# A decode step of attention beside a gated MLP, with gradients: the MLP's w2 in 18 blocks of 96 rows, and the first head's loads and products ahead of the MLP

## The chip, the cores and the metric

The kernel runs on one core of a Trainium2 chip, in one launch. The metric is the time of one execution on the device in microseconds (us). Three runs of the kernel before took 762.09, 760.68 and 760.85 us; the median is 760.85 us.

## The reference, cut to what matters

One token (`Sq = 1`, width `D = 640`) passes a layer norm without gain. Two branches read the result and are added to the input: attention over a cache of 8192 keys and values for each of 32 heads of width 128, and a gated MLP of inner width `F = 1728`. The kernel returns the output and the gradients with respect to the input, both caches and all five weights. All arrays are bfloat16.

```python
def _fwd_reference(A_x, A_k_cache, A_v_cache, A_wq, A_wo, B_x, B_w1, B_w3, B_w2):
    xn = _layernorm(A_x)
    q = (xn @ wq)                                  # 32 heads of 128
    p = softmax(q . k_cache * 128 ** -0.5)         # 8192 keys a head
    attention = (p . v_cache) @ wo
    h = silu(xn @ w1) * (xn @ w3)                  # 1728 wide
    return A_x + attention + h @ w2
# reference(): out, and the vjp of it with grad_out for
#   A_x, A_k_cache, A_v_cache, A_wq, A_wo, B_w1, B_w3, B_w2
```

With one token every weight gradient is an outer product of two vectors, and so is the gradient of each head's K and V. The kernel therefore reads every large array once and writes an array of the same size for each: 151.34 MB in and 151.34 MB out by the profile.

## The kernel before

Every large tile in SBUF has 128 partitions; a head's K or V is one tile of 2 MB (128 partitions of 64 rows of 128 values). The work is in three stretches.

Setup. `x_row` and `g_row` are loaded, constants are made, and the layer norm is done. `nc.sync` (the SP queue) issues all loads in the order of the program: w1 (L142), w3 (L144), w2 in three parts (L149), then `load_wq(0)` (L130), `load_wo(0)` (L137), `load_k(0)` (L108), `load_v(0)` and `load_v(1)` (L114).

The gated MLP, `mlp_steps()`, a generator that stops once at its `yield`. In the first part TensorE forms gate and up as 16 + 16 columns of `gu_ps` (L448: for each of w1 and w3, 16 blocks of 108 columns by 5 chunks of 128 rows, each block being the stationary operand). VectorE multiplies each part of w2 with the gradient (`T2`, L459), TensorE adds it up over pieces of 64 columns with an identity (`dh_ps`, L462), and VectorE ends the sum (L455). A chain of small operations on `sm_f` gives the gradients of gate and up; `diag` (L486) spreads them over a diagonal. Between the two parts the kernel runs `prep_steps(0)`, which makes q and the gradient of the attention output for the first four heads (`qs_g`, `do_g`). In the second part a product with ones turns `diag` into rows that all partitions hold (`bc_sb`, L496 to L502). Then four things follow: the MLP output (L509), the gradient of w2, written over `w2c` by ScalarE (L511) and stored by `nc.gpsimd` (the POOL queue, L512); the products of w1 and w3 with `bc_sb` for the gradient of x (`T`, L518, summed by L521); and the gradients of w1 and w3, which VectorE writes over the weights themselves (L524) before POOL stores them (L528).

The heads. The loop runs from -1 to 31. In iteration h the next head n = h + 1 gets its scores and its products with V: `product(n, "S", 0/1)` and `product(n, "DP", 0/1)`, each half a VectorE product (L333) and eight matmuls with the identity that add it up (L335); `row_max` and `exps` between them. The current head c = h gets its probabilities (`probs`), its outer products (`outer`, L342 on VectorE and L346 on ScalarE, each stored by POOL, L348), `attend`, `dscores` and its share of the weight gradients. For iteration -1 only the part for head 0 runs. `load_v(h + 2)` and `load_k(h + 3)` stand inside the loop.

The order on VectorE, ScalarE, SP and POOL is the order of the program (`manual_schedule`); TensorE's instructions are placed by the scheduler and then run in that order. What the loads must wait for is set by the pools:

- `kpool` has three buffers. They hold w1, w3 and K of head 0 first. `load_k(1)` takes the buffer of w1, and so it waits until the gradient of w1, which stands in that buffer, has been stored. `load_k(2)` waits in the same way for the store of the gradient of w3.
- `vpool` has two buffers, for V of heads 0 and 1. `load_v(2)` waits until head 0 is done with V.
- `opool` has seven buffers: the three parts of w2, `diag`, `bc_sb`, and later the outer products `ot`.
- `tpool` has two buffers, for all products that TensorE sums up (`T2`, `T13` and `T`).

The order at the start of the loop before the change is:

```python
        mlp = mlp_steps()
        next(mlp)
        for _ in prep_steps(0):
            pass
        for _ in mlp:
            pass
        load_k(1)
        load_k(2)
        prev = None
        for h in range(-1, H):
```

Of the kernel before, what the change touches and what calls it, by code (L numbers as in the profile page):

```python
# [9 lines left out]
BF16 = mybir.dt.bfloat16  # L10
F32 = mybir.dt.float32
# [5 lines left out]
P = 128  # L17
# [4 lines left out]
def kernel(  # L22
# [22 lines left out]
    nc = tc.nc  # L45
# [3 lines left out]
    D = A_x.shape[2]  # L49
# [8 lines left out]
    ORDERED = {mybir.EngineType.DVE, mybir.EngineType.SP, mybir.EngineType.Pool, mybir.EngineType.Activation}  # L58
    GW = 8
    HB = GW // GH  # L60
    R2 = 16
    FR = F // R2
    ACT_J = 8
    assert H % GW == 0 and GW % GH == 0 and F % R2 == 0 and FR <= P and P % GH == 0
# [8 lines left out]
    opool = ctx.enter_context(tc.tile_pool(name="op", bufs=7))  # L73
# [16 lines left out]
    w1_v = B_w1.rearrange("(p ci) f -> p ci f", ci=NC)  # L90
# [6 lines left out]
    with tc.manual_schedule(engines=ORDERED):  # L97
# [8 lines left out]
        def load_k(h):  # L106
            Kt = kpool.tile([P, J, DH], BF16, name="Kt", tag="K")
            nc.sync.dma_start(Kt[:], kc[h])  # L108
            kv_tiles[h] = kv_tiles.get(h, [None, None])
            kv_tiles[h][0] = Kt  # L110

        def load_v(h):
            Vt = vpool.tile([P, J, DH], BF16, name="Vt", tag="V")
            nc.sync.dma_start(Vt[:], vc[h])  # L114
            kv_tiles[h] = kv_tiles.get(h, [None, None])
            kv_tiles[h][1] = Vt
# [22 lines left out]


        w1t = kpool.tile([P, NC, F], BF16, name="w1t", tag="K")
        nc.sync.dma_start(w1t[:], w1_v)  # L142
        w3t = kpool.tile([P, NC, F], BF16, name="w3t", tag="K")
        nc.sync.dma_start(w3t[:], w3_v)  # L144
        w2_parts = []
        r0 = 0
        for rows in (6, 5, 5):
            w2c = opool.tile([P, rows, D], BF16, name="w2c", tag="o")
            nc.sync.dma_start(w2c[0:FR], w2_v[:, r0:r0 + rows, :])  # L149
            w2_parts.append((r0, rows, w2c))  # L150
            r0 += rows
        assert r0 == R2
        load_wq(0)
        load_wo(0)
        load_k(0)
        load_v(0)
        load_v(1)


# [277 lines left out]
                steps.append(finish_steps(st.g))  # L437


        def mlp_steps():  # L440
            DRUN = 64
            DR1 = 96
            assert F % DR1 == 0 and D % DRUN == 0
# [44 lines left out]
                                    .to_broadcast([FR, 2, R2, FR // 2, 2]),  # L488
                                    dgu2[0:FR].unsqueeze(3).to_broadcast([FR, 2, R2, FR // 2, 2]), ALU.mult)
            bc_sb = opool.tile([P, 2, F], BF16, name="bc_sb", tag="o")  # L490
            yield
            RC = 4
            for wi in range(2):
                for r0 in range(0, R2, RC):
                    bc_ps = ps_w.tile([P, RC, FR], F32, name="bc_ps", tag="w")
                    nc.tensor.matmul(bc_ps[:], lhsT=ones_bf[0:FR, :],  # L496
                                     rhs=diag[0:FR, wi, r0:r0 + RC].rearrange("p r a b -> p r (a b)"), start=True, stop=True)
                    part = bc_sb[:, wi, r0 * FR:(r0 + RC) * FR].rearrange("p (r q) -> p r q", r=RC)
                    if wi == 0 and r0 % (2 * RC) == 0:
                        nc.vector.tensor_copy(part, bc_ps[:])  # L500
                    else:
                        nc.scalar.copy(part, bc_ps[:])  # L502
# [32 lines left out]
            if steps and next(steps[0], "end") == "end":  # L535
                steps.pop(0)

        mlp = mlp_steps()
        next(mlp)
        for _ in prep_steps(0):  # L540
            pass
        for _ in mlp:
            pass
        load_k(1)
        load_k(2)
        prev = None
        for h in range(-1, H):
            n = new_head(h + 1) if h + 1 < H else None
            c = hs.pop(h) if h >= 0 else None
            if h >= 0:  # L550
                g, hh = divmod(h, GH)
            if h == H - 2:
                for dst, src in late:
                    store(dst, src)
            if n:
                product(n, "S", 0)
            if c:
                probs(c)
                outer(c, c.do, c.P2, c.Pf, dvc, h, 0)
                if prev:  # L560
                    keep_dq(prev)
                gap()
                row_dots(c)
                attend(c)
                turn_wq(c)
            if n:
                product(n, "S", 1)
            if c:
                outer(c, c.do, c.P2, c.Pf, dvc, h, 1)
                if h + 2 < H:  # L570
                    load_v(h + 2)
                gap()
                dscores(c)
                outer(c, c.q, c.U2, c.Uf, dkc, h, 0)
                keep_wq(c)
            if n:
                row_max(n)
                product(n, "DP", 0)
            if c:
                outer(c, c.q, c.U2, c.Uf, dkc, h, 1)  # L580
                if h + 3 < H:
                    load_k(h + 3)
                gap()
            if n:
                exps(n)
                product(n, "DP", 1)
            if c:
                weights(c)
                gap()
                if hh == 0 and g + 1 < NG:  # L590
                    if (g + 1) % HB == 0:
                        load_wq((g + 1) // HB)
                    load_wo(g + 1)
                if hh == 1 and g + 1 < NG:
                    steps.append(prep_steps(g + 1))
                    gap()
                if hh == 2:
                    gap()
            prev = c
        keep_dq(prev)  # L600
        while steps:
            gap()
# [58 lines left out]
```

## Time and profile before

| What | Value |
|---|---|
| Median of three runs | 760.85 us |
| The profiled execution's own time | 761.41 us |
| Its span, first to last instruction | 759.4 us |
| PE (matmuls) busy | 557.3 us, 73% of the span |
| DVE (VectorE) busy | 632.5 us, 83% |
| ACT (ScalarE) busy | 474.4 us, 62% |
| POOL (GpSimd) busy | 87.5 us, 12% |
| Moved by DMA | 303.72 MB, mean 400 GB/s |
| Mean granted TensorE clock | 0.79 of full speed |
| Loads of w1 and w3 | 2160 KB each |
| Loads of w2 | 810 + 675 + 675 KB |
| Loads of wq (eight heads) and wo (four heads) | 1280 KB and 640 KB |
| Load of one head's K or V | 2048 KB |

The span lies 2.0 us under the execution's own time. A busy share is a mean over the three stretches, which have different limits; the stretches are seen in the page's row of 40 slices, of about 19 us each. A timeline gives for each group of instructions its start, the time to the end of the group, the engine ("SPq" and "POOLq" are queues that issue transfers, "PEld" is TensorE's loading of a stationary operand), the line, and what it reads and writes.

### The profile page before, as it was taken

Reading aid. Unit: us, or ns where it says so; the run is one execution under the profiler, and the core shown is the slowest. Engines: PE = TensorE matmul, PEld = TensorE weight load, DVE = VectorE, ACT = ScalarE, POOL = GpSimd, SP = SyncE. Lnnn points to the kernel's source line nnn. Section 1 sums busy time; section 2 is a strip of 40 time slices with the busy share of each in tenths; the row PEclk is TensorE's granted clock in tenths of the full one; section 3 lists DMA queues with packets and bytes.
Section 4 is the critical chain, followed back from the end, with each engine's and each line's share of the span. In section 5 each row is a group of like instructions: output and inputs, shape, how many; then the busy total and the mean of one; then the engine's idle time right before and its main releaser. Section 6 shows DMA issues by size and latency. Waiting matters only on the chain.

```text
span 759.4 us, 15976 instructions
## 1 busy us (share of the span) xinstructions
PE 557.3 (73%) x6528; PEld 337.3 (44%) x6543; DVE 632.5 (83%) x706; ACT 474.4 (62%) x1421; POOL 87.5 (12%) x166
## 2 busy tenths in 40 slices
PE   6865888878688773877777765788786778777860
PEld 5652445544454442544443433444353445444440
DVE  2577999999799894998788994999887998899970
ACT  2180567777666763787655963778564957677672
POOL 0010011111001120110100120111000111011120
PEclk9987778787886687787896987777795888877665
DMA  8969799999999999999999999999999999999795
GB/s 298 335 258 366 301 428 425 423 422 418 430 427 428 423 416 426 426 423 417 429 428 426 426 377 430 424 427 419 430 425 427 428 418 427 428 427 424 325 363 201
DMA packets 37355, 303.72 MB, mean 400 GB/s; under 512 B 4120, under 2 KB 5874, under 8 KB 12194
## 3 DMA queue, kind: packets, MB, share of 16 engines
q1 hardware_dynamic: 15190, 151.35, 48.5%
q0 software_dynamic: 22080, 151.35, 48.4%
q8 instruction: 51, 0.84, 0.4%
q14 instruction: 22, 0.18, 0.1%
q10 hardware_dynamic: 12, 0.00, 0.0%
HBM read 151.34 MB, written 151.34 MB: 399 GB/s over the span
## 4 chain that ended last, share of the span: by engine, by line
DMA 55%; DVE 31%; PE 6%; issue 4%; ACT 2%; SPq 1%; POOL 0%; POOLq 0%; DVEq 0%; ACTq 0%
DMA out_dram<-ot 39%; DVE T L333 14%; DVE ot L342 11%; DMA out_dram<-wo_g 9%; DMA wo_g<-in_A_wo_dram 4%; DMA w2c<-in_B_w_dram 3%; PE psS L335 2%; ACT ot L346 1%; DVE S_sb L352 1%; DVE DP_sb L386 1%; PE psDP L335 1%; PE dx_ps L521 1%; DVE w3t L524 1%; DVE T L518 1%; SPq L149 0%
## 5 line engine op out<-in xcount | busy, mean ns | idle before, releaser
L335 PE MATMUL psDP<-T,ident_bf 128*128 128x512 bf16 x512 | 187.2, 529 | 65.3 <-DVE T L333 65.3
L335 PEld LDWEIGHTS <-ident_bf 128*128 128x128 bf16 x1024 | 120.2, 120 | 221.8 <-issue 167.0
L346 ACT ACTIVATE ot<-qs_g,Uf 128x128 bf16<-128x128 bf16 x512 | 156.4, 389 | 68.6 <-DMA out_dram<-ot 55.9
L346 ACT ACTIVATE ot<-do_g,Pf 128x128 bf16<-128x128 bf16 x512 | 156.3, 389 | 13.4 <-DMA out_dram<-ot 12.5
L333 DVE TENSOR_TENSOR T<-Kt,qs_g 128x4096 bf16<-128x4096 bf16 x64 | 146.4, 2289 | 2.4 <-PE psDP L335 1.3
L335 PE MATMUL psS<-T,ident_bf 128*128 128x512 bf16 x512 | 141.2, 426 | 9.4 <-DVE T L333 9.4
L333 DVE TENSOR_TENSOR T<-Vt,do_g 128x4096 bf16<-128x4096 bf16 x64 | 146.0, 2281 | 1.4 <-DMA Vt<-in_A_v_cache_dram 1.4
L342 DVE TENSOR_TENSOR ot<-qs_g,U 128x3072 bf16<-128x3072 bf16 x64 | 112.2, 1753 | 40.5 <-DMA out_dram<-ot 40.5
L348 POOL DMA_DIRECT2D out_dram<-ot x128 | 68.2, 533 | 546.3 <-ACT ot L346 192.8
L342 DVE TENSOR_TENSOR ot<-do_g,P 128x3072 bf16<-128x3072 bf16 x64 | 112.3, 1755 | 4.5 <-DMA out_dram<-ot 3.4
L399 PEld LDWEIGHTS <-Kt 128*128 128x128 bf16 x2048 | 57.2, 97 | 12.0 <-issue 9.3
L399 PE MATMUL ob<-U,Kt 128*128 128x1 bf16 x2048 | 57.2, 164 | 2.5 <-issue 1.2
L379 PEld LDWEIGHTS <-Vt 128*128 128x128 bf16 x2048 | 57.1, 97 | 0.0
L379 PE MATMUL ob<-P,Vt 128*128 128x1 bf16 x2048 | 56.9, 163 | 0.0
L365 PEld LDWEIGHTS sm<-rsum,ones_f 128*128 128x128 f32 x64 | 16.4, 282 | 52.7 <-ACT E L364 47.2
L364 ACT ACTIVATE E<-S_sb,negM 128x64 f32<-128x64 f32 x32 | 11.0, 343 | 44.8 <-DVE negM L361 44.7
L245 ACT COPY woT<-ps_t 128x512 bf16<-128x512 bf16 x40 | 22.8, 576 | 25.9 <-PE ps_t L240 25.9
L418 ACT ACTIVATE dq_diag<-ident_bf,odq 128x128 bf16<-128x128 bf16 x32 | 12.8, 399 | 41.2 <-DVE odq L414 41.2
L356 PE MATMUL sm<-ident_f,mrow 128*128 128x128 f32 x64 | 17.6, 361 | 23.8 <-DVE mrow L354 23.0
L373 ACT ACTIVATE Pf<-E,rZ 128x16 f32<-128x16 f32 x32 | 9.8, 307 | 39.2 <-DVE rZ L369 39.2
L352 DVE TENSOR_REDUCE S_sb<-psS 128x64 f32<-128x512 f32 x32 | 21.9, 685 | 11.2 <-PE psS L335 11.2
L262 PE MATMUL ps_d<-woT,G_rep 128*128 128x512 bf16 x33 | 13.4, 405 | 22.6 <-ACT woT L245 22.6
(145 smaller groups left out, 542.4 us busy)
## 6 DMA issues: line engine op xcount, KB each, us to landing
out_dram<-ot POOLq DMA_DIRECT2D x128, 1024.0 KB, 28.4
Kt<-in_A_k_cache_dram SPq DMA_DIRECT2D x32, 2048.0 KB, 17.6
Vt<-in_A_v_cache_dram SPq DMA_DIRECT2D x32, 2048.0 KB, 14.0
wq_g<-in_A_wq_dram SPq DMA_DIRECT2D x4, 1280.0 KB, 24.2
wo_g<-in_A_wo_dram SPq DMA_DIRECT2D x8, 640.0 KB, 9.9
out_dram<-wo_g POOLq DMA_DIRECT2D x8, 640.0 KB, 23.9
out_dram<-wq_g POOLq DMA_DIRECT2D x15, 256.0 KB, 20.4
w1t<-in_B_w_dram SPq DMA_DIRECT2D x1, 2160.0 KB, 8.3
```

The lines of the kernel that those rows point to most:

```text
L245: nc.scalar.copy(woT[:], ps_t[:])
L262: nc.tensor.matmul(ps_d[:], lhsT=G_rep[:, ci, :], rhs=woT[:], start=(ci == 0), stop=(ci == NC - 1))
L333: nc.vector.tensor_tensor(T[:], src[:, :, ds_], vec[:, ds_].unsqueeze(1).to_broadcast([P, J, DHH]), ALU.mult)
L335: nc.tensor.matmul(ps[:], lhsT=ident_bf[:], rhs=T[:, :, RUN * i:RUN * (i + 1)], start=(half == 0 and i == 0), stop=(half == 1 and i == DHH ...
L342: nc.vector.tensor_tensor(ot[:, 0:JD], vec.rearrange("p (a b) -> p a b", b=2).unsqueeze(1).to_broadcast([P, JD, DH // 2, 2]), w2[:, j0:j0 ...
L346: nc.scalar.activation(ot[:, j].rearrange("p a b -> p (a b)"), vec, ACTF.Copy, scale=wf[:, half, j - JD:j - JD + 1])
L348: nc.gpsimd.dma_start(dst[h][:, j0:j0 + JH, :], ot[:].rearrange("p j a b -> p j (a b)"))
L352: nc.vector.tensor_reduce(st.S[:], st.ps["S"][:], AX.X, ALU.add)
L356: nc.tensor.matmul(st.sm[:, 8:8 + P], lhsT=mrow[:].to_broadcast([P, P]), rhs=ident_f[:], start=True, stop=True, skip_group_check=True)
L365: nc.tensor.matmul(st.sm[:, 3:4], lhsT=ones_f[:], rhs=rsum[:], start=True, stop=True, skip_group_check=True)
L379: mm = nc.tensor.matmul(st.ob[:, 0:1], lhsT=st.V[:, j, :], rhs=st.P2[:, j, 0:1], start=(j == 0), stop=(j == J - 1), skip_group_check=True)
L399: nc.tensor.matmul(st.ob[:, 1:2], lhsT=st.K[:, j, :], rhs=st.U2[:, j, 0:1], start=(j == 0), stop=(j == J - 1), skip_group_check=True)
```

## The change

w2 is cut into 18 blocks of 96 rows in place of 16 blocks of 108, so its tiles have 96 partitions; its three parts hold 6 blocks each. The blocks of w1 and w3 in L448 become 96 columns wide. The order of the first loads on the SP queue becomes wq, wo, K of head 0, V of head 0, w2, w1, w3, V of head 1. `prep_steps(0)` and iteration -1 of the head loop (the products and exponents of head 0) come ahead of the MLP, which is one plain function now; the loads of K for heads 1 and 2 follow it as before.

```diff
-    R2 = 16
+    R2 = 18
     FR = F // R2
...
         w1t = kpool.tile([P, NC, F], BF16, name="w1t", tag="K")
-        nc.sync.dma_start(w1t[:], w1_v)
         w3t = kpool.tile([P, NC, F], BF16, name="w3t", tag="K")
-        nc.sync.dma_start(w3t[:], w3_v)
-        w2_parts = []
-        r0 = 0
-        for rows in (6, 5, 5):
-            w2c = opool.tile([P, rows, D], BF16, name="w2c", tag="o")
-            nc.sync.dma_start(w2c[0:FR], w2_v[:, r0:r0 + rows, :])
-            w2_parts.append((r0, rows, w2c))
-            r0 += rows
-        assert r0 == R2
         load_wq(0)
         load_wo(0)
         load_k(0)
         load_v(0)
+        w2_parts = []
+        RP = 6
+        assert R2 % RP == 0
+        for r0 in range(0, R2, RP):
+            w2c = opool.tile([P, RP, D], BF16, name="w2c", tag="o")
+            nc.sync.dma_start(w2c[0:FR], w2_v[:, r0:r0 + RP, :])
+            w2_parts.append((r0, RP, w2c))
+        nc.sync.dma_start(w1t[:], w1_v)
+        nc.sync.dma_start(w3t[:], w3_v)
         load_v(1)
...
-        def mlp_steps():
+        def mlp():
...
             bc_sb = opool.tile([P, 2, F], BF16, name="bc_sb", tag="o")
-            yield
-            RC = 4
             for wi in range(2):
-                for r0 in range(0, R2, RC):
-                    bc_ps = ps_w.tile([P, RC, FR], F32, name="bc_ps", tag="w")
+                for k, (r0, n) in enumerate(((0, 5), (5, 5), (10, 4), (14, 4))):
+                    bc_ps = ps_w.tile([P, n, FR], F32, name="bc_ps", tag="w")
...
-        mlp = mlp_steps()
-        next(mlp)
         for _ in prep_steps(0):
             pass
-        for _ in mlp:
-            pass
-        load_k(1)
-        load_k(2)
         prev = None
         for h in range(-1, H):
...
             prev = c
+            if h < 0:
+                mlp()
+                load_k(1)
+                load_k(2)
```

## The prediction

> **What bounds the kernel now.** I read the page's row of 40 slices first.
>
> ```profile
> DMA  8969799999999999999999999999999999999795
> GB/s 298 335 258 366 301 428 425 423 422 418 430 427 428 423 416 426 426 423 417 429 428 426 426 377 430 424 427 419 430 425 427 428 418 427 428 427 424 325 363 201
> ```
>
> From the sixth slice (95 us) to the 37th the transfers run at about 425 GB/s with a busy share of 9 tenths or more: there the kernel is bound by moving bytes. Only the first five slices and the last three fall short. The first five carry 298 + 335 + 258 + 366 + 301 = 1558 where 5 x 425 = 2125 would fit; the missing 567 x 19 us / 425 are some 25 us. The change touches only this stretch, so I read next the table of windows there (busy time of PE, PEld, DVE, ACT, POOL; granted clock; DMA share; GB/s).
>
> ```profile
> 2.00:12.00 10.00, 5.08 (x53) 4.33 (x54) 4.07 (x17) 4.15 (x6) 0.00 (x0) 1.00 0.99 389
> 14.00:28.00 14.00, 14.00 (x126) 12.91 (x126) 4.09 (x3) 0.00 (x0) 0.00 (x0) 1.00 1.02 233
> 28.00:40.00 12.00, 8.54 (x54) 5.41 (x54) 7.80 (x18) 5.37 (x10) 0.00 (x0) 1.00 1.03 424
> 46.00:58.00 12.00, 7.13 (x78) 6.75 (x76) 10.67 (x6) 7.51 (x11) 3.52 (x4) 0.84 0.62 193
> 58.00:80.00 22.00, 12.93 (x53) 5.41 (x51) 16.72 (x10) 0.44 (x2) 0.57 (x1) 0.70 0.99 385
> ```
>
> The last row is left for what follows. From 14 to 28 us, when w2 lands, the DMA is busy but moves only 233 GB/s; from 46 to 58 us it has too little to do; from 58 to 80 us it is full. Then the SP queue's own waits up to 200 us, and the timeline of the first 85 us:
>
> ```profile
> SPq L108 <- DMA out_dram<-w1t: 42.4, 1, 42.4
> SPq L108 <- DMA out_dram<-w3t: 7.2, 1, 7.2
> ```
>
> ```profile
> 16.89 7.59 PEld L448 LDWEIGHTS <-w3t 128*108 128x108 bf16 x80
> 30.98 1.52 PE L462 MATMUL dh_ps<-T,ident_bf 108*108 108x320 bf16 x10 [1.01 <-DVE T L459]
> 40.42 3.82 DVE L518 TENSOR_TENSOR T<-w1t,bc_sb 128x3456 bf16<-128x3456 bf16 x2
> 41.02 1.85 PEld L509 LDWEIGHTS <-w2c 108*128 108x128 bf16 x65
> 54.74 0.57 POOL L528 DMA_DIRECT2D out_dram<-w1t  x1
> 62.84 4.48 DVE L333 TENSOR_TENSOR T<-Kt,qs_g 128x4096 bf16<-128x4096 bf16 x2
> 66.06 7.99 SPq L108 DMA_DIRECT2D Kt<-in_A_k_cache_dram  x2
> 78.11 2.29 DVE L333 TENSOR_TENSOR T<-Kt,qs_g 128x4096 bf16<-128x4096 bf16 x1 [1.26 <-PE psDP L335]
> ```
>
> The load of K of head 1 waits 42.4 us for the store of the gradient of w1, whose buffer it takes. That store is issued at 54.74 us, the load at 66.06 us. Meanwhile (62.84 to 78.11 us) VectorE does head 0's products. At 78.11 us head 1's first product starts, without a wait for its K. So those 15.3 us of products lie beside the stores of both gradients and the loads of K, while the DMA is full: they cost little.
>
> **My measure.** From head 1's first product on, both programs do the same with the same buffers, and V of head 1 and both gradients of w1 and w3 are out of the way or in flight. The change in time is the shift of this instant, S1 (78.11 us before). DMA-bound or not, what follows moves with it.
>
> **The change part by part.**
>
> *Loads.* In MB the new order is wq 1.31, wo 0.66, K 2.10, V 2.10, w2 2.21, w1 2.21, w3 2.21, V 2.10. The first 10 us at 389 GB/s move 3.89 MB, to 12.0 us; K of head 0 needs 4.07 MB, so 12.4 us. V (6.17 MB) at 424 GB/s ends at 17.4 us. For w2 in 96 partitions no row exists. Its 2.21 MB take 5.2 us at 424 GB/s and 9.5 us at the 233 GB/s of its own stretch; pieces of 1280 bytes stay, so I take 8 us, nearer the slow end: 25.4 us. w1 and w3 add 5.2 us each: 30.6 and 35.8 us. A landing is counted by its last piece; w3 lands in the trace at 1.55 + 14.0 = 15.6 us, where the bytes alone give 13.4, so the lag is 0 to 2.2 us; I take 1. K 13.4, w1 31.6, w3 36.8 us.
>
> The Trainium skill ("DMA: Bandwidth & Descriptors", section "Why a DMA increments its semaphore by 16 and not by 1") says that a transfer is spread over the largest number up to 16 of engines that divides the outer dimension: 12 for 108 partitions, 16 for 96. By it w2 would take 9.5 x 12/16 = 7.1 us and the sum would be 0.9 us lower; it speaks for this part of the change.
>
> *Head 0 first.* `prep_steps(0)` (5.4 us of ACT, before at 33 to 39 us) now lies under the load of K; without that cover it would be 5 us more. The products took from 62.84 us to the end of the last psDP matmul at 81.2 us, 18.3 us; from 13.4 us that gives 31.7 us, when w1 lands. The Exp table (1.28 us) is hidden behind VectorE's products.
>
> *MLP front, TensorE.* In the order of the changed program TensorE has, after head 0: 90 matmuls of w1, 21 of dh, 90 of w3, 9 of dh. Before, the 160 gate and up matmuls lay under the slow load of w2; now w1 and w3 land last and nothing is left to cover them. Their pitch is 7.59 us / 80 = 95 ns with 108 columns; L509 with 128 columns goes at 1.85/65 = 28 ns. 96 columns has no row: 28 and 95 ns bound it; being a width other than 128, I take 95 x 96/108 = 85 ns. 90 are 7.65 us. One dh matmul of 384 is 1.52/10 x 384/320 = 0.18 us. Step by step: w1 to 39.4; 20 dh to 43.0; meanwhile the third w2 product needs the first dh group's buffer (41.2), the reduction (0.56) and itself (2.16, as the first had): 43.9, its first dh matmul 44.1; w3 to 51.8; 9 dh 53.4; reduction 54.0. From the copy of gate and up to the first `T` of L518 were 32.94 to 40.42, 7.5 us, with a ScalarE copy (`do_g`, 1.3 us) in the way that is now gone: 7.0. The new blocks of `bc_ps` (5, 5, 4, 4) change copies by under 0.1 us. L518 starts at 61.0 us, 20.6 later than 40.42.
>
> The skill's page "TensorE: Matmul & The Clock Gate" (section "Weight-path perf modes — Fast Weight Load (FWL) and DoubleRow") gives the fast weight load to 128 columns alone, which speaks against a gain at 96; its formula of columns / 1.2 GHz would make 80 ns, and the sum 0.9 us lower.
>
> *MLP tail.* VectorE's 22.4 us (40.42 to 62.84) stay. POOL stores w1's gradient behind the three of w2, which wait for ScalarE: 18 scalings in place of 16, 2 x 0.73 us more. So 54.74 - 40.42 + 1.5 = 15.8 us after L518: 76.8 us. The 10 more L509 matmuls (0.3 us) lie under VectorE.
>
> *The wait that now shows.* K of head 1 needs the stores of both gradients ahead of it on the engines: 2.21 + 2.21 + 2.10 MB at 385 GB/s are 16.9 us, some 2 more until the first piece: 19 us after the issue. From above, K was there by 78.11, 23.4 us after. I take 21: S1 = 97.8 us. VectorE is done with the MLP at 61.0 + 22.4 = 83.4 and idles 14 us, queued behind this product: `probs`, `outer` and with them all stores of head 0, V of head 2 on SP. The DMA has nothing from 41 us (V of head 1 landed) to the first w2 store at some 67 us.
>
> **Sum.** S1 moves by 97.8 - 78.1 = 19.7, say 20 us. Span 759.4 + 20 = 779.4; own time 761.41 + 20 = 781.4; that execution lies 0.6 us above the median 760.85, so 781 us. With the ends (w2 -2.8 / +1.5, matmul pitch 80 to 95 ns -0.9 / +1.8, lag 1, K -2 / +2.4) the case reaches from 774 to 787.
>
> **Rivals.**
> (a) *Weights of 96 columns load fast.* For: 28 ns at L509. Against: 95 ns at L448 and width alone differs. 90 matmuls take 2.5 us; 5.15 x 2 = 10.3 less: S1 moves 9.5 us, 770.
> (b) *w2 stays slow, or TensorE is throttled when the MLP starts.* For: the granted clock was 0.70 from 58 to 80 us, 1.00 in the 108-column matmuls. w2 as slow as its whole 14 us is 6 more: 787; a clock of one half for both sets of 90 would add up to 15.
> (c) *Faster: bytes alone decide.* The 14 us at 233 GB/s moved 3.26 MB, which need 7.7 us at 424: 6.3 less, 754.5. It holds if computing never starves the DMA, so S1 by 71.8 and L518 by 35.0 us, before w3 has landed (36.8). Merely to break even L518 must start by 41.3. For it speaks that 15.3 us of products leave the stretch after the MLP; against it that they were covered there.
>
> **How the numbers follow.** Main case 0.73, (a) 0.10, (b) 0.12, (c) 0.04, something that ends level 0.01. Under 0.2% (1.5 us) a measurement of this kernel cannot tell from no change. Slower 0.95, same 0.01, faster 0.04. The time is the main case's 781; the range of 769 to 788 takes in (a) and the near end of (b).
>
> **What would show it.** In the new profile: w2 at over 233 GB/s; L447 (gate and up) at 80 to 95 ns; L515's first `T` near 61 us; POOL's store of w1's gradient near 77; VectorE idle some 14 us until K lands; head 1's first product near 98; a hole in the DMA from about 42 to 66 us. It is wrong if that product starts before 80 us, or if the later stretch does not move with it.

## The result, and the profile after

The changed kernel takes 786.38 us (784.18 to 787.23, 4 runs), the kernel before 761.32 us beside it; the ratio is 1.0324, with a 95% interval of 1.0299 to 1.035. The profiled execution took 787.23 us, its span is 785.1 us, 25.7 us longer than before. The page's row of 40 slices (19.6 us each) of the changed kernel:

```profile
DMA  8921889999999999999999999999999999999896
GB/s 322 318 120 39 319 332 419 424 425 423 420 429 427 429 421 420 427 427 422 418 428 429 423 415 394 428 429 425 417 433 427 426 422 415 427 427 414 342 366 201
```

Only the first six slices differ much; the third and fourth (39 to 78 us) are nearly empty; I call that stretch the hole. The timeline of the changed kernel (start, time to the end of the group, engine, line, operation):

```profile
16.26 4.49 DVE L332 TENSOR_TENSOR T<-Kt,qs_g 128x4096 bf16<-128x4096 bf16 x2 [8.68 <-DMA Kt<-in_A_k_cache_dram]
...
38.30 7.36 PE L447 MATMUL gu_ps<-xn_col_bf,w1t 128*96 128x1 bf16 x90 [8.09 <-DMA w1t<-in_B_w_dram]
...
45.52 6.45 PE L461 MATMUL dh_ps<-T,ident_bf 96*96 96x384 bf16 x21
...
51.81 5.29 PE L447 MATMUL gu_ps<-xn_col_bf,w3t 128*96 128x1 bf16 x90
...
56.96 3.09 PE L461 MATMUL dh_ps<-T,ident_bf 96*96 96x384 bf16 x9
...
67.23 3.83 DVE L515 TENSOR_TENSOR T<-w1t,bc_sb 128x3456 bf16<-128x3456 bf16 x2 [0.17 <-ACT bc_sb L499]
...
82.85 0.58 POOL L525 DMA_DIRECT2D out_dram<-w1t  x1
...
92.63 7.03 SPq L108 DMA_DIRECT2D Kt<-in_A_k_cache_dram  x2
...
103.84 2.29 DVE L332 TENSOR_TENSOR T<-Kt,qs_g 128x4096 bf16<-128x4096 bf16 x1 [13.71 <-DMA Kt<-in_A_k_cache_dram]
```

The first `T` of w1 stands at 67.23 us (40.42 before). VectorE idles 13.71 us for K of head 1, and head 1's first product, S1, starts at 103.84, 25.73 us later than before. The SP queue's waits up to 200 us of the changed kernel (total, times, longest, us) show the load of K of head 1 waiting 69.8 us for the store of w1's gradient, in place of 42.4:

```profile
SPq L108 <- DMA out_dram<-w1t: 69.8, 1, 69.8
SPq L108 <- DMA out_dram<-w3t: 6.3, 1, 6.3
```

The same six stretches of both traces follow (busy time of PE, PEld, DVE, ACT, POOL; granted clock; DMA share; GB/s). Before:

```profile
0.00:20.00 20.00, 13.08 (x139) 12.33 (x140) 5.31 (x25) 4.86 (x6) 1.14 (x8) 1.00 0.85 295
20.00:41.00 21.00, 17.26 (x130) 12.87 (x131) 12.56 (x23) 6.37 (x12) 0.00 (x0) 1.00 1.05 354
41.00:60.00 19.00, 13.00 (x186) 12.28 (x183) 16.07 (x8) 12.51 (x19) 3.52 (x4) 0.82 0.69 237
60.00:80.00 20.00, 12.05 (x33) 4.64 (x33) 14.72 (x10) 0.44 (x2) 0.57 (x1) 0.67 0.99 388
80.00:100.00 20.00, 16.17 (x187) 9.20 (x185) 19.58 (x24) 12.15 (x41) 2.13 (x4) 0.82 0.81 310
100.00:120.00 20.00, 16.79 (x187) 9.30 (x187) 19.72 (x21) 12.92 (x45) 2.13 (x4) 0.83 1.00 424
```

After:

```profile
0.00:20.00 20.00, 9.53 (x63) 5.33 (x64) 8.77 (x26) 9.38 (x13) 1.14 (x8) 1.00 0.87 320
20.00:41.00 21.00, 9.43 (x65) 5.55 (x63) 10.39 (x8) 0.44 (x2) 0.00 (x0) 0.83 1.05 328
41.00:60.00 19.00, 19.00 (x179) 15.43 (x179) 3.17 (x3) 0.00 (x0) 0.00 (x0) 0.59 0.20 86
60.00:80.00 20.00, 11.89 (x158) 9.45 (x157) 15.93 (x22) 14.05 (x23) 1.63 (x2) 0.63 0.18 51
80.00:100.00 20.00, 5.55 (x54) 5.25 (x54) 9.30 (x5) 1.83 (x3) 1.85 (x3) 0.71 0.92 342
100.00:120.00 20.00, 11.17 (x153) 6.45 (x153) 15.98 (x17) 10.46 (x34) 1.60 (x3) 0.67 0.83 324
```

I call the *lost DMA time* of a stretch its length times (1 - rate/425), 425 GB/s being the rate of the full stretch. Before it is 6.1 + 3.5 + 8.4 + 1.7 + 5.4 + 0.0 = 25.2 us; after, 4.9 + 4.8 + 15.2 + 17.6 + 3.9 + 4.8 = 51.2. The difference is 25.9 us, and the span grew by 25.7. Of these 25.9 us, 22.6 lie between 41 and 80 us, where the changed kernel has soon loaded all that it may load and has for long nothing to store (the windows of 5 us from 50 to 75 us show 0 to 5 GB/s); 4.7 lie behind 100 us; between 80 and 100 us, where VectorE idles for K, the DMA is at 0.92 and loses less than before.

So two measures fit: the shift of S1, which the prediction used, and the lost DMA time. That the second one fits is in part bookkeeping: every kernel here but e9 moves the same bytes, so its span is these bytes at 425 GB/s plus all its lost DMA time, and the table only adds that what is lost later hardly differs. Which of the two prices a wait rightly is told by the experiments that move S1 and the lost DMA time by different amounts (e6, e10, e12). This table has all twelve experiments, below the change; shifts of the profiled span, of lost DMA time up to 120 us (160 us for the contiguous w2) and of S1 are against the kernel before, in us.

| Kernel | Time, ratio [interval] | Span | Lost DMA time | S1 |
|---|---|---|---|---|
| the change | 786.38, 1.0324 [1.0299, 1.035] | +25.7 | +25.9 | +25.7 |
| e1 blocks only | 760.30, 0.9996 [0.9985, 1.0007] | -0.1 | -0.6 | -0.5 |
| e2 order only | 786.39, 1.0328 [1.0305, 1.0352] | +25.7 | +26.3 | +26.1 |
| e3 loads first only | 788.89, 1.0367 [1.0348, 1.0385] | +27.9 | +27.7 | +27.9 |
| e4 products first only | 794.93, 1.0444 [1.0417, 1.0472] | +35.3 | +34.1 | +35.4 |
| e5 w2 contiguous | 813.34, 1.0695 [1.0674, 1.0717] | +50.9 | +52.2 | +51.9 |
| e6 K's own buffer | 782.90, 1.0301 [1.0269, 1.0333] | +20.4 | +17.4 | +12.6 |
| e7 w2's store later | 787.27, 1.0347 [1.032, 1.0375] | +23.4 | +23.8 | +21.1 |
| e8 half the products | 760.32, 0.9997 [0.9987, 1.0006] | -1.0 | -1.2 | -1.2 |
| e9 w2 in 128 partitions | 782.99, 1.0287 [1.0269, 1.0305] | +22.4 | +20.9 | +22.6 |
| e10 K in place of V | 783.28, 1.0298 [1.0281, 1.0314] | +22.1 | +23.0 | +13.4 |
| e11 added matmuls | 765.89, 1.0067 [1.0055, 1.008] | +4.7 | +4.9 | +4.7 |
| e12 hole filled | 757.05, 0.9938 [0.9924, 0.9952] | -2.7 | -3.5 | +0.8 |

(e9 moves 0.74 MB more, 1.7 us at 425 GB/s; with them its 20.9 are 22.6.)

### The profile page after: what moved, and what is told of

Read it like the earlier page. It is cut to its first block, busy times and chain, and to the rows that moved or that the text cites. A ratio compares the mean times of both kernels' runs of the same rounds, so it can differ in the third digit from the quotient of the medians.

```text
span 785.1 us, 16039 instructions
## 1 busy us (share of the span) xinstructions
PE 556.6 (71%) x6559; PEld 335.7 (43%) x6573; DVE 633.2 (81%) x706; ACT 476.3 (61%) x1423; POOL 86.9 (11%) x166
## 4 chain that ended last, share of the span: by engine, by line
DMA 51%; DVE 33%; issue 9%; PE 3%; ACT 1%; POOL 0%; SPq 0%; POOLq 0%; DVEq 0%; ACTq 0%
DMA out_dram<-ot 29%; DVE T L332 15%; DVE ot L341 13%; DMA out_dram<-wo_g 10%; DMA Kt<-in_A_k_cache_dram 4%; DMA wo_g<-in_A_wo_dram 4%; DMA w2c<-in_B_w_dram 3%; PE psS L334 2%; DVE S_sb L351 1%; DMA out_dram<-w1t 1%; DVE DP_sb L385 1%; ACT ot L345 1%; DVE U L393 1%; DVE P L370 0%; PE psDP L334 0%
## 5 line engine op out<-in xcount | busy, mean ns | idle before, releaser
L334 PE MATMUL psDP<-T,ident_bf 128*128 128x512 bf16 x512 | 175.2, 501 | 68.1 <-DVE T L332 68.1
L334 PE MATMUL psS<-T,ident_bf 128*128 128x512 bf16 x512 | 147.1, 439 | 25.4 <-DVE T L332 25.3
L345 ACT ACTIVATE ot<-do_g,Pf 128x128 bf16<-128x128 bf16 x512 | 156.4, 389 | 13.6 <-DMA out_dram<-ot 12.7
L398 PEld LDWEIGHTS <-Kt 128*128 128x128 bf16 x2048 | 57.3, 98 | 12.6 <-issue 10.0
L364 PEld LDWEIGHTS sm<-rsum,ones_f 128*128 128x128 f32 x64 | 14.2, 242 | 49.6 <-ACT E L363 44.7
L351 DVE TENSOR_REDUCE S_sb<-psS 128x64 f32<-128x512 f32 x32 | 21.9, 685 | 12.4 <-PE psS L334 12.4
L239 PE MATMUL ps_t<-ident_bf,wo_g 128*128 128x128 bf16 x160 | 17.7, 243 | 17.9 <-DMA wo_g<-in_A_wo_dram 17.6
L363 ACT ACTIVATE E<-S_sb,negM 128x64 f32<-128x64 f32 x32 | 11.0, 344 | 32.0 <-DVE negM L360 31.9
## 6 DMA issues: line engine op xcount, KB each, us to landing
Vt<-in_A_v_cache_dram SPq DMA_DIRECT2D x32, 2048.0 KB, 13.4
```

The lines of the kernel that those rows point to most:

```text
L239: nc.tensor.transpose(ps_t[:, hh * DH:(hh + 1) * DH], wo_g[:, hh, ci * P:(ci + 1) * P], ident_bf[:])
L334: nc.tensor.matmul(ps[:], lhsT=ident_bf[:], rhs=T[:, :, RUN * i:RUN * (i + 1)], start=(half == 0 and i == 0), stop=(half == 1 and i == DHH ...
L345: nc.scalar.activation(ot[:, j].rearrange("p a b -> p (a b)"), vec, ACTF.Copy, scale=wf[:, half, j - JD:j - JD + 1])
L351: nc.vector.tensor_reduce(st.S[:], st.ps["S"][:], AX.X, ALU.add)
L364: nc.tensor.matmul(st.sm[:, 3:4], lhsT=ones_f[:], rhs=rsum[:], start=True, stop=True, skip_group_check=True)
L398: nc.tensor.matmul(st.ob[:, 1:2], lhsT=st.K[:, j, :], rhs=st.U2[:, j, 0:1], start=(j == 0), stop=(j == J - 1), skip_group_check=True)
```

## The experiments

### The parts of the change, one by one (e1 to e4)

**Blocks only.** The kernel before with

```diff
-    R2 = 16
+    R2 = 18
...
-        for rows in (6, 5, 5):
+        for rows in (6, 6, 6):
```

and the matching pieces of `bc_ps`.

> The kernel before with w2 in 18 blocks of 96 rows and nothing else. Theory (the order costs the time, the blocks help): w2 lands some 4 to 5 us sooner than the 29.1 us of before, the first T of the w1 products starts 4 to 5 us before 40.42 us, head 1's first product moves by the same from 78.11 us, and the time falls to 756 to 757.5 us. Rival (pieces of 1280 bytes set the pace of w2, not the number of partitions): w2 lands within 1 us of before and the time stays at 760 to 762 us. Second rival (the blocks cost part of the 25 us, by narrower weights and more scalings): 764 us or more.

The time stayed: 760.30. By the packets w2 took 10.2 us from the end of w3 (15.2 to 25.4 us) in place of 13.4 (14.8 to 28.2), but the third product of w2 did not follow. The timeline of this kernel:

```profile
24.03 5.73 PE L462 MATMUL dh_ps<-T,ident_bf 96*96 96x384 bf16 x20
...
27.96 2.14 DVE L459 TENSOR_TENSOR T<-w2c,g_bc_bf 96x3840 bf16<-96x3840 bf16 x1
...
30.15 1.79 PE L462 MATMUL dh_ps<-T,ident_bf 96*96 96x384 bf16 x10 [0.39 <-DVE T L459]
```

The product stands on VectorE behind the first reduction, which waited 2.49 us for the dh matmuls and starts at 27.48, and it reuses the `T` buffer that the same matmuls read. So it starts at 27.96, with TensorE and not the data as its limit; `T` of w1 comes at 39.71 (40.42), and two more scalings push the store of w1's gradient to 55.34 (54.74).

**Order only.** The changed kernel with 16 blocks of 108 rows:

```diff
-    R2 = 18
+    R2 = 16
...
-        for r0 in range(0, R2, RP):
+        for rows in (6, 5, 5):
```

> The changed kernel with the old 16 blocks of 108 rows: the new order of loads and products alone. Theory (the order costs all of it): w2 on 108 partitions lands later, and so do w1 and w3 behind it, by some 4 us; the first T of the w1 products starts at 70 to 72 us against 67.23, head 1's first product at 107 us, 788 to 791 us. Rival (the blocks carry the loss): back to 765 us or less.

786.39: the whole loss is the order's, and the blocks neither cost nor bring anything that can be measured in either order.

**Loads first only.** 18 blocks and the new order of loads, with the MLP still ahead of `prep_steps(0)` and the products:

```diff
         w1t = kpool.tile([P, NC, F], BF16, name="w1t", tag="K")
-        nc.sync.dma_start(w1t[:], w1_v)
         w3t = kpool.tile([P, NC, F], BF16, name="w3t", tag="K")
-        nc.sync.dma_start(w3t[:], w3_v)
...
+            nc.sync.dma_start(w2c[0:FR], w2_v[:, r0:r0 + RP, :])
...
+        nc.sync.dma_start(w1t[:], w1_v)
+        nc.sync.dma_start(w3t[:], w3_v)
         load_v(1)
```

> 96-row blocks, the loads in the new order, but the MLP ahead of the products of head 0 as in the kernel before. Theory: w1 and w3 land at 38 and 43 us as in the changed kernel, nothing covers gate and up, the first T starts at about 66 us, the products of head 0 follow the MLP and end near 104 us, beside the stores and the load of K of head 1; head 1's first product at 103 to 105 us, 784 to 787 us, the same as the changed kernel, since the products were covered in either place. Rival (putting the products ahead of the MLP is what costs): 770 us or less. Second rival (putting them ahead gained their 15 us, and the loads cost 40): 800 us.

788.89, S1 at 106.00. With the loads in the new order, doing the products ahead is worth 2.2 us of S1 and 2.5 us of time (788.89 to 786.38). With the MLP first, the new order of the loads costs 28.6 us (760.30 to 788.89).

**Products first only.** 18 blocks and the old order of loads (w1, w3, w2, then wq, wo, K, V), with the products ahead of the MLP:

```diff
         w1t = kpool.tile([P, NC, F], BF16, name="w1t", tag="K")
+        nc.sync.dma_start(w1t[:], w1_v)
         w3t = kpool.tile([P, NC, F], BF16, name="w3t", tag="K")
+        nc.sync.dma_start(w3t[:], w3_v)
...
         load_wq(0)
...
-        nc.sync.dma_start(w1t[:], w1_v)
-        nc.sync.dma_start(w3t[:], w3_v)
         load_v(1)
```

> 96-row blocks, the loads in the old order (w1, w3, w2, then wq, wo, K, V), but the products of head 0 ahead of the MLP. Theory: TensorE runs gate and up while it waits, but VectorE's work of the MLP now stands behind K and V of head 0, which land last, at about 33 and 38 us; the first T of the w1 products starts at 63 to 68 us, head 1's first product some 36.6 us after it, 100 to 105 us, 782 to 787 us. Rival (the order of the loads alone makes the loss): 755 to 762 us.

794.93, worse than expected: now the MLP, whose weights are there early, waits in VectorE's and TensorE's order behind products whose loads come late (first product at 35.61 us, `T` at 76.91, S1 at 113.51). A second cause stands in the timeline: on TensorE the 142 last gate and up matmuls run ahead of the 16 that add up head 0's scores (from 48.36 us), and VectorE idles 14.58 us until these are done:

```profile
54.69 0.69 DVE L352 TENSOR_REDUCE S_sb<-psS 128x64 f32<-128x512 f32 x1 [14.58 <-PE psS L335]
```

How much of the loss is due to this placement by the scheduler was not tried. The two parts of the order do not add up either: each alone costs more (788.89, 794.93) than both together (786.38).

### What head 0's products cost before (e8)

```diff
+            if first and half == 1:
+                return
```

in `product` of the kernel before, with `first` set for head 0 alone.

> The kernel before, with the second half of head 0's S product and of its DP product left out (two VectorE products of 2.2 us and their 16 matmuls; the scores of head 0 are sums over half the width only). It asks what the products of head 0 cost where they stood before the change, that is, what moving them ahead could win at most. Theory (they lie beside the stores of w1's and w3's gradients and the load of K for head 1, so that the end of the wait for K hardly moves): head 1's first product starts at 76.5 to 78.1 in place of 78.11, time 759 to 761. Rival (VectorE's and TensorE's work on head 0 is what sets that start): start about 71 to 74, time 753.5 to 757.

The time is 760.32, the ratio 0.9997: 4.6 us of VectorE and 16 matmuls taken away bring nothing that can be measured. The timeline shows why:

```profile
76.93 2.29 DVE L335 TENSOR_TENSOR T<-Kt,qs_g 128x4096 bf16<-128x4096 bf16 x1 [5.67 <-DMA Kt<-in_A_k_cache_dram]
```

VectorE is ready 5.67 us ahead of this product and waits for K of head 1. Without that half, S1 comes 1.2 us earlier and stands at the landing of K (0.9 of the 1.2 us stand already in the store of w1's gradient, which is issued at 53.84 us here and at 54.74 before): before the change the products stood in the shadow of the transfers, and to do them elsewhere wins no more than that where K comes no sooner.

### What the wait for K is worth (e6, e7, e10)

**A buffer of its own for K of head 1.** The changed kernel with

```diff
-    kpool = ctx.enter_context(tc.tile_pool(name="kp", bufs=3))
+    kpool = ctx.enter_context(tc.tile_pool(name="kp", bufs=4))
...
-    opool = ctx.enter_context(tc.tile_pool(name="op", bufs=7))
+    opool = ctx.enter_context(tc.tile_pool(name="op", bufs=5))
```

> The changed kernel with four buffers for K in place of three, and five for the outer products in place of seven to make room. K of head 1 then no longer waits for the store of w1's gradient (issued at 82.85 us). Theory (the wait for that buffer is what stands ahead of head 1, and the later stretch follows its start): VectorE's idle 13.7 us ahead of head 1's first product goes, that product starts at about 90.2 in place of 103.84, and the time falls by up to 13.7 to about 773, plus what two fewer buffers for the outer products cost (span less that start, 681.2 us in all kernels so far, would grow by it). Rival (bytes decide: only the 2 MB of K that now fill the hole, some 5 us at 420 GB/s, are won): start about 90, but time about 781, the later stretch longer by the rest. Second rival (K of head 1 lands in the hole, but VectorE still waits, for V or for the MLP's end): start above 98, time above 780.

S1 falls by 13.2 us, to 90.68, and VectorE's wait is gone; the time falls by 3.5, to 782.90. The lost DMA time up to 120 us is 8.5 us less than in the changed kernel (K fills part of the hole: 197 GB/s from 41 to 60 us). Some 8.6 us come back between 120 and 650 us, where this kernel moves 422, 413 and 415 GB/s and the changed one 425, 421 and 425 (windows of 180, 200 and 150 us):

```profile
300.00:500.00 200.00, 137.13 (x1694) 82.12 (x1696) 156.42 (x169) 121.28 (x372) 21.89 (x41) 0.78 0.99 413
500.00:650.00 150.00, 116.20 (x1342) 67.52 (x1345) 136.07 (x147) 105.51 (x322) 16.85 (x32) 0.77 1.00 415
```

I put that down to the two missing outer-product buffers: in the whole run VectorE and ScalarE waited 61.9 and 79.0 us for stores of outer products, 38.3 and 58.8 in the changed kernel. Fewer buffers alone were not tried. The span is 5.3 us shorter, so some 5 us are won back behind 650 us; from what, stays open.

**K and V of head 1 exchanged.** To remove the wait without touching the number of buffers:

```diff
+            pool, tag = (vpool, "V") if h == 1 else (kpool, "K")
-            Kt = kpool.tile([P, J, DH], BF16, name="Kt", tag="K")
+            Kt = pool.tile([P, J, DH], BF16, name="Kt", tag=tag)
...
-        load_v(1)
+        load_k(1)
```

and the reverse for V of head 1.

> The changed kernel with the buffers of head 1's K and V exchanged: K of head 1 is loaded early, into V's second buffer, and V of head 1 takes the buffer of w1 after its gradient is stored. Bytes, buffers and their number stay. Theory (the wait of K of head 1 for the store of w1's gradient is worth its whole 13.7 us, and the later stretch moves with head 1's first product; the loss with the K buffer of its own came from the two outer-product buffers that it took): head 1's first product starts at about 90.2, V of head 1 lands at 102 to 104 where its first product wants it at about 102, time 773 to 776. Rival (the transfers decide what follows: the stores and loads behind the MLP are as late as before): start at 90, time 781 or more.

The rival is right. The timeline of this kernel:

```profile
91.49 2.28 DVE L334 TENSOR_TENSOR T<-Kt,qs_g 128x4096 bf16<-128x4096 bf16 x1
...
108.01 2.29 DVE L334 TENSOR_TENSOR T<-Vt,do_g 128x4096 bf16<-128x4096 bf16 x1 [4.31 <-DMA Vt<-in_A_v_cache_dram]
```

S1 is 12.4 us earlier, with the same bytes and buffers, and the time only 3.1 us shorter (783.28). Even the product with V, which waits 4.31 us, comes some 8 us sooner than in the changed kernel (S1 + 12 us there). Head 4's first product still comes 7.1 us sooner than in the changed kernel (152.91 and 160.02 us), yet only 3.6 us of that are left at the end of the span. The lost DMA time up to 120 us fell by 2.9 us (4.2 less from 100 to 120 us, at 413 GB/s in place of 324, and 1.3 more elsewhere). VectorE's idle 13.7 us were worth the DMA time that they left empty, some 3 to 4 us.

**w1's gradient stored ahead of w2's last part**, on the POOL queue of the changed kernel:

```diff
-                nc.gpsimd.dma_start(dw2_v[:, r0:r0 + rows, :], w2c[0:FR])
+                if r0 + rows < R2:
+                    nc.gpsimd.dma_start(dw2_v[:, r0:r0 + rows, :], w2c[0:FR])
...
                 nc.gpsimd.dma_start(dst, wt[:])
+                if wi == 0:
+                    nc.gpsimd.dma_start(dw2_v[:, r0:r0 + rows, :], w2c[0:FR])
```

> The changed kernel with one thing moved on the POOL queue: the store of the last part of w2's gradient is issued behind the store of w1's gradient in place of ahead of it. In the changed kernel VectorE had written w1's gradient by 79.2 us, and the store was issued at 82.85, behind that part. Theory (POOL's order costs 3.6 us, and the load of K for head 1 follows the store's issue by 7 us plus 11 us of transfer): head 1's first product starts at 100.2 to 100.8 in place of 103.84, time 783. Rival (the load of K is paced by the stores' bytes, not by the issue, or w1's gradient is ready only at 82.8): start 103 to 104, time 786.

S1 falls by 4.6 us to 99.21, more than the theory had it (1.0 of it stands already in the first `T`, 66.23 us, ahead of the edit); the time, 787.27, does not fall. The profiled span is 2.3 us shorter, but the ratio's interval (1.032 to 1.0375) holds that of the change: no gain is shown.

### Why w1 landed late (e5, e9)

**Contiguous pieces.**

```diff
-    w2_v = B_w2.rearrange("(r q) c -> q r c", r=R2)
+    w2_v = B_w2.rearrange("(q r) c -> q r c", r=R2)
```

> The changed kernel with w2 and its gradient seen as (q r) c in place of (r q) c: each partition then holds one contiguous piece of 7680 bytes of w2 per part, in place of six pieces of 1280 bytes. Blocks, order and work stay. In the changed kernel the stretch of w2's load moved 218 to 259 GB/s, no more than the 16-block form did, and w1 landed at 38.3 us against a forecast of 31.6. Theory (the 1280-byte pieces set the pace, the number of partitions doesn't): w2 lands about 4 us sooner, w1 at about 34, and the start of head 1's first product (103.84 us in the changed kernel) falls by about 4 to 100, time about 782. Rival (the partitions, 96 of 128, set the pace, or the load shares the queue with something else): w1 at 38, start 103.8, time 786.

Neither: the rate is the rival's, the time is nobody's. w2's packets of 7680 bytes took 0.516 us each, and the windows from 20 to 25 and from 25 to 30 us moved 227 and 256 GB/s (218 and 259 in the changed kernel); w1's first matmul came 1.7 us sooner. But the blocks of w1 and w3 are strided columns now, and TensorE pays for that:

```profile
36.56 16.31 PE L447 MATMUL gu_ps<-xn_col_bf,w1t 128*96 128x1 bf16 x90 [5.63 <-DMA w1t<-in_B_w_dram]
...
59.12 16.15 PE L447 MATMUL gu_ps<-xn_col_bf,w3t 128*96 128x1 bf16 x90
```

181 ns a matmul in place of 82; with the rest of the strided work, the hole lasts to 100 us, and the time is 813.34. Piece size was not what made w2 slow. The window from 20 to 25 us, for the next experiment:

```profile
20.00:25.00 5.00, 3.87 (x15) 1.54 (x14) 2.12 (x4) 0.00 (x0) 0.00 (x0) 0.88 0.98 227
```

**128 partitions.**

```diff
-            nc.sync.dma_start(w2c[0:FR], w2_v[:, r0:r0 + RP, :])
+            nc.sync.dma_start(w2c[:], B_w2[r0 * 80:r0 * 80 + P * RP, :].rearrange("(p r) c -> p r c", r=RP))
```

> The changed kernel with each part of w2 loaded as 128 partitions of one contiguous 7680-byte piece (rows 0 to 767, 480 to 1247 and 960 to 1727, which overlap) in place of 96 partitions: 2.95 MB in place of 2.21. The work uses the first 96 partitions as before, so the MLP's sums over w2 are of the wrong rows. Contiguous 7680-byte pieces on 96 partitions had moved some 230 GB/s, just as the 1280-byte ones. Theory (tiles of fewer than 128 partitions load slowly): 2.95 MB at 425 GB/s take 6.9 us in place of 9.4; w1's first gate matmul starts at about 35.9 in place of 38.30, head 1's first product at about 101.4 in place of 103.84, time about 784. Rival (w2's place in memory or what runs beside it sets the pace): 2.95 MB at 235 GB/s take 12.5 us; w1's first matmul at 41.5, head 1's first product at 107, time about 789.5.

The theory is right. The window from 20 to 25 us of the changed kernel, in which w2 is loaded,

```profile
20.00:25.00 5.00, 2.84 (x13) 1.09 (x11) 2.99 (x4) 0.00 (x0) 0.00 (x0) 1.00 1.08 218
```

and of this one:

```profile
20.00:25.00 5.00, 3.22 (x15) 1.29 (x13) 2.99 (x4) 0.00 (x0) 0.00 (x0) 1.00 1.00 417
```

The DMA is as busy in both and moves almost twice as much; a packet of 7680 bytes takes 0.295 us. (The parts are also read as one whole stretch of memory here. That is not what made them fast: wq's pieces of 2048 bytes, with gaps between them and on 128 partitions, took 0.084 us each (median) in the changed kernel, 24 GB/s an engine.) The first gate matmul starts at 33.67 us in place of 38.30, although a third more of w2 is read; without the added 0.74 MB it would stand at some 31.9 (an estimate, 1.7 us at 425 GB/s). So 96 partitions cost some 6.4 us here. The time is 3.4 us shorter, as is the span (3.3).

### TensorE's pace (e11)

The kernel before with 18 blocks and, after every ten gate and up matmuls, one idle matmul:

```diff
+            def warm():
+                tc.keep_in_program_order(nc.tensor.matmul(
+                    accbank[:, 64:512], lhsT=ident_bf[:], rhs=XN_rep[:].rearrange("p a b -> p (a b)")[:, 0:448],
...
+                    if r % 2 == 1:
+                        warm()
```

> The kernel before with the 18 blocks of 96 rows and one idle matmul of 448 columns after every ten gate and up matmuls, 18 in all, into unused columns. With the blocks alone w2 landed 2.8 us sooner, but its third product then waited for the dh matmuls, that is for TensorE, and the time stayed at 760.3. Theory (TensorE is slow in the gate and up matmuls because the clock is not granted to so light a load): their pitch falls from some 82 ns to 30 to 60, the third product of w2 starts at about 26 in place of 27.96, the first T at 37 to 38.5 in place of 39.71, head 1's first product at 75 to 76.5 in place of 77.62, time 757.5 to 759. Rival (weights of 96 columns load slowly at any clock): the pitch stays at 80 or more, the 18 added matmuls cost 4 to 8 us of TensorE, the first T moves to 40 to 43, time 760 to 764.

The rival is right: ten gate matmuls still take some 0.93 us, in every one of the full groups from 14 to 29 us, and each added matmul puts 0.19 us between two groups. One of them:

```profile
14.09 0.93 PE L454 MATMUL gu_ps<-xn_col_bf,w1t 128*96 128x1 bf16 x10
```

`T` of w1 moves to 45.68 us and S1 to 82.82; 765.89 us, a little worse than the rival had it. The theory of a clock kept up by added work falls: the granted clock is shown as 1.00 in the windows from 10 to 25 us of the kernel with the blocks alone already, at 82 ns a matmul.

### The hole filled (e12)

The kernel before, with two loads moved:

```diff
         load_v(1)
+        load_wq(1)
+        load_wo(1)
...
-                if hh == 0 and g + 1 < NG:
-                    if (g + 1) % HB == 0:
+                if hh == 0 and 0 < g and g + 1 < NG:
+                    if (g + 1) % HB == 0 and g > 1:
```

> The kernel before with one thing moved: the loads of the second wq part (1.31 MB) and of the second wo part (0.66 MB), whose buffers are free from the start, are issued right behind V of head 1 in place of some 90 and 180 us later. Nothing else changes. In the kernel before the DMA moved only 152 GB/s from 45 to 50 us, 220 from 50 to 55 and 272 from 55 to 60. Theory (what the change lost, and what is there to win, is DMA time with nothing to move; bytes put into such a hole shorten the later full stretch by what they take there, whatever head 1's first product does): 1.97 MB at 425 GB/s, up to 4.6 us less, time 756 to 758, with head 1's first product still at 77.5 to 79. Rival (the later stretch moves with head 1's first product alone): time 760 to 761. Second rival (the added loads delay the stores of the gradients of w2 and w1 and with them K of head 1): head 1's first product at 80 or later, time 761 or more.

757.05 us against 761.19 of the kernel before beside it, ratio 0.9938 [0.9924, 0.9952]: 4.1 us less by the medians and 4.7 by the ratio, and faster than both kernels. In the kernel before the two loads were issued at 165.52 and 89.87 us. The windows of this kernel:

```profile
41.00:60.00 19.00, 15.07 (x177) 14.09 (x174) 15.96 (x8) 12.13 (x18) 3.53 (x4) 0.64 0.93 344
60.00:80.00 20.00, 9.95 (x36) 4.08 (x36) 13.68 (x10) 0.44 (x2) 0.57 (x1) 0.83 0.95 367
```

and its S1:

```profile
78.88 2.29 DVE L335 TENSOR_TENSOR T<-Kt,qs_g 128x4096 bf16<-128x4096 bf16 x1 [2.80 <-DMA Kt<-in_A_k_cache_dram]
```

From 41 to 60 us it moves 344 GB/s in place of 237, 4.8 us of DMA time; 1.0 us is given back in the next window, where K of head 1 comes 0.8 us later. S1 did not move forward at all, and yet the time fell: the later stretch does not move with S1, it ends when the bytes are through. One rival is left: the edit also takes a load of wq out of the full stretch near 165 us, and what that is worth by itself was not tried.

## Why the prediction was right, and where it was not

- *What bounds the kernel.* Right, and more so than the prediction used: in twelve of the thirteen rows of the table the shift of the span is that of the lost DMA time within 1.4 us (e9 with its added bytes counted; e6, with fewer buffers later, is the exception at 3.0). One slice was misread: the 24th, at 377 GB/s, falls short too.
- *"The change in time is the shift of this instant, S1 ... DMA-bound or not, what follows moves with it."* For this pair it gave the right number (25.73 and 25.7 us), because a late MLP delays the stores, the hole and S1 alike; that the wrong currency gave the right sum was in this sense luck. As a rule it fell: e10 moved S1 by 12.4 us for 3.1 us of time, e12 lost 0.8 us of S1 and won 4 to 5.
- *The wait that takes the place of the removed one.* Place and length were right: POOL's store 15.6 us after `T` (forecast 15.8), S1 21.0 us after that store (21), VectorE idle 13.7 us (14). Its price was not: 3 to 4 us in e10. The cost lay in the hole that the prediction saw ("nothing from 41 us ... to some 67 us"; it lasted to 73.5 us, when the first w2 store was issued) but did not put into its sum.
- *The size, 781 against 786.4.* The first `T` was mis-sized, 61.0 against 67.23 us. By the starts of the rows: w1's first matmul +6.7, w1's 90 matmuls -0.6, dh +1.6, w3's 90 -2.5, last dh +1.5, chain -0.5.
- *w1's +6.7 us.* The first 20 us moved 320 GB/s where the prediction took 389 and 424 (+1.9). w2 and w1 took 2.1 us more by the windows' bytes, 218 GB/s from 20 to 25 us and 259 from 25 to 30 where "over 233" was forecast. The first matmul came 3.7 us after the bytes, not 1 (+2.7). By e9, 96 partitions cost 6.4 us; the prediction had put in 2.8 of them (8 us for w2 in place of 5.2). So some 3.6 of the 6.7 us are theirs, and some 3 are left for the first loads and the landing.
- *dh at 0.18 us.* It came from the last ten matmuls of the trace before; the first twenty there took 5.54 us, 0.28 each, and were the nearer row. After, they took 0.31 (6.45 / 21) and 0.34 us (3.09 / 9), at a granted clock of 0.50 in the windows from 45 to 50 and from 55 to 60 us (0.84 between them).
- *Gate and up at 85 ns.* 82 ns for w1 (7.36 / 90), so rival (a), fast loads of 96 columns, is out; w3's took 59, which no term had.
- *Rival (b), 787.* Its time was nearly met, but by several small terms: w2 was slow and dh was slow. Its second condition held, a granted clock of 0.50 from 35 to 50 us, but did not have its price: w1's 90 matmuls took the 82 ns that they take at 1.00 (blocks only), and w3's took less.
- *Rival (c), bytes alone, 754.5.* It had the right currency, and its own condition, that computing never starves the DMA, failed: from 50 to 75 us hardly anything moved.
- *w2 in 8 us.* The bound of 9.5 us went by 233 GB/s as "its own stretch". By the packets that was the rate of all loads there: wq started at 17.8 us, wo at 22.8 and K at 25.5, and w2 itself took 13.4 us, 165 GB/s.

Weighed in the prediction was the rule of the Trainium skill ("DMA: Bandwidth & Descriptors", section "Why a DMA increments its semaphore by 16 and not by 1") that 108 partitions use 12 engines and 96 use 16. The runs agree with it as a ratio: 10.2 us with 96 partitions to 13.4 with 108 are 0.76, and 12/16 is 0.75. The agreement is loose, because wq and wo moved beside w2 in the kernel before, from 17.8 us on, and no trace here names the engines. The 7.1 us worked out from it were wrong because the 9.5 us under them were: 12/16 of 13.4 are 10.1.

The page "SBUF — State Buffer" (section "Door 1: The DMA port swizzle") says that a transfer's rate depends on how many of SBUF's 16 ports its partitions reach, eight partitions to a port. By its table 96 partitions reach all 16, eight of them by four partitions only; an estimate from it, with its 435 GB/s for all 16, is that two thirds of the bytes go through half the ports, some 326 GB/s at best. e9 agrees in kind (417 GB/s as soon as all 128 take part), but the 218 measured are well below, and the measurement decides; no run here shows the ports themselves.

## What to carry to other kernels

Where most of a kernel runs at the full DMA rate, price a change of order by the DMA time that it leaves empty, stretch by stretch, and not by the wait of a compute engine: a 13.7 us stall of VectorE cost 3 to 4 us, while the 39 us around the hole, from 41 to 80 us, lost 22.6. What is loaded first should be what the first stores depend on, and what has a free buffer belongs into the hole. Before giving up an order, ask what covered the work that one wants to move: products that were already hidden brought 2.5 us, and the order of the loads that went with them cost 28.6.

## What the hardware showed unexpectedly

- Loads of w2 into 96 partitions ran at some 14 GB/s an engine, half the pace of a full tile: w2's 10.2 us in 96 partitions are 13.6 GB/s an engine if all 16 take part (a DMA busy share of 1.12 and 1.09 in the windows from 15 to 25 us there), a 7680-byte packet in 0.516 us is 14.9, and one in 0.295 us on 128 partitions is 26.0. In sum, the window from 20 to 25 us, nearly all of it w2, moved 218 GB/s into 96 partitions with pieces of 1280 bytes and 227 with pieces of 7680; into 128 partitions with 7680-byte pieces it moved 417, with the DMA about as busy. Stores did not show it: w2's gradient left the same 96 partitions by the POOL queue in packets of 5120 bytes with a median of 0.212 us, 24 GB/s an engine (the change).
- Gate and up matmuls of one column kept 82 ns with 96 weight columns at a granted clock shown as 1.00 (blocks only, 7.4 us for 90) and as 0.50 (the change, w1), but took 52 to 61 ns for w3, behind the dh matmuls, in the change, e3, e6, e7 and e10 (74 in e9). What sets this pace stays open. Strided weight columns took 181 ns.
- dh matmuls of 384 columns took 0.29 us right behind gate and up and 0.18 a few us later, with the clock shown as 1.00 in both (blocks only).
